# Channel mixing in f16 with the identity folded into the weights, in a sliding-window attention kernel

## The chip, the cores and the metric

The kernel runs on one core of a Trainium2 chip. The metric is the device time of one execution in microseconds (us), the median of several runs. The kernel before takes 632.37 us (3 runs, 632.07 to 632.75).

## The reference

```python
def _attn_ref(q, k, v):                  # 8 batches, 8 heads, 576 tokens, 64 wide
    scores = scale * np.matmul(q, k.transpose(0, 1, 3, 2))
    scores = np.where(mask, scores + bias[None], -1000000000.0)   # band of 128 keys
    ...
    return np.matmul(attn, v)

def _moe_ref(x, w_theta, w_tok_r, w_tok_i, w_ch):                 # x: 8 x 576 x 512
    theta = x @ w_theta
    zr, zi = x * np.cos(theta), x * np.sin(theta)
    y = einsum('ts,bsd->btd', w_tok_r, zr) + einsum('ts,bsd->btd', w_tok_i, zi)
    u = x + y
    return u + np.maximum(u @ w_ch, 0.0)
```

The change concerns the last two lines: u, and the mixing over channels u @ w_ch.

## The kernel before, in words

All data are f32, and each product is made of parts: an operand is split into a high part and the rest (`_hi`, `_lo`), and hi x hi, hi x lo and lo x hi are added up in PSUM. The mixing over tokens uses f16 parts, scaled by powers of two so that they stay in f16's range; the mixing over channels uses f32 parts (type F32R), with no scale.

The work goes by batches. For batch b the main loop calls `attend(b + 1)`, the attention of the next batch, and then `turn(b + 1)`, which turns that attention's result `x_sb` into the tiles `z_hi`, `z_lo`. Between their pieces it places the work that batch b still has:

- `mix` (generator, line 694): mixing over tokens, 8 groups of 27 matmuls 128x288 (in the text: token matmuls). When a group is done, DVE adds it to x (L717, giving u in `xtf`), ACT makes `u_hi` (L719) and POOL makes `u_lo` (L721). The POOL subtractions are kept in `lows` and issued behind the DVE instruction that ends `Head.ready` (L425).
- `channels` (generator, line 737): mixing over channels, 8 **channel groups** of 12 matmuls 128x288: 4 with `wch_hi`,`u_hi`, 4 with `wch_lo`,`u_hi`, 4 with `wch_hi`,`u_lo`. DVE computes max(product, 0) + u (L749) and a DMA writes it out.

`attend` has four steps g = 0 to 3, one per pair of heads. In each, PE computes the scores of a pair four ahead (`ps<-kh,qh`), DVE adds the bias with a custom instruction (L491), ACT takes the exponential (L494), ACT and DVE split the result into f16 parts `hl` (L519, L522), and a DMA transposes them to `pt`. DVE also makes the low parts of the next q and k (L402, L404). PE then multiplies a pair that was prepared before by its values (`ps<-vh,pt`, 54 matmuls), and DVE divides (`finish`, L555 to L560, giving `x_sb`). `turn` transposes `x_sb` (`ps<-fixed,x_sb`, 4 per tile, 5 tiles), splits it (L599 to L606), multiplies by `wth` (theta, 8 or 12 matmuls of 128x512), and DVE, ACT and POOL compute sine, cosine and z.

A channel group is placed at g = 2 and g = 3 of `attend` (for b = 1, the first call, only at g = 3), and six more in `turn`, by `between()`. PE executes its instructions in the program's order (`pinned`); the order on DVE, ACT and POOL comes from a scheduler with a model of the time, so the tables below show it.

The weights of `channels` are loaded late, in `attend(1)`: `unpack(LATE)`, four chunks of 128x512, each decoded (L184 to L193) and split (`split`: ACT L220, POOL L221).

`spread_from` and `spread_to` find the largest value over all partitions: PE transposes a column (L100), DVE takes the maximum and puts it on a diagonal, and PE sends it to all partitions by a matmul with ones. `scales_first` and `batch_scale` derive from it the scales of z.

Of the kernel before, what the change touches and what calls it, by code (L numbers as in the profile page):

```python
# [999 lines left out]
```

## Time and profile before

| what | value |
|---|---|
| median of 3 runs | 632.37 us (632.07 to 632.75) |
| the profiled execution's own time | 630.07 us |
| its span | 628.3 us |
| PE busy | 606.7 us (97%), 5724 matmuls |
| DVE busy | 506.7 us (81%) |
| ACT busy | 482.7 us (77%) |
| POOL busy | 129.9 us (21%) |
| mean granted clock of TensorE | 0.986 of full speed |

The span is from the first to the last instruction; the execution's own time has 1.8 us more. Busy times of different engines overlap. A row of a timeline gives the start in us from the span's beginning, the duration, the engine, the line, the operation, the tiles (out<-in) with partitions and elements, how many instructions it puts together, and in brackets how long the engine had been idle and what ended that. Matmuls are pipelined, so the start of one and the start of the next tell the pace, not the duration of one.

### The profile page before, as it was taken

How to read it: one execution, taken by the hardware profiler on the slowest of the kernel's cores; microseconds unless marked ns; L12 is line 12 of the kernel's file. 1: busy time of each engine (PE TensorE's matmuls, PEld its weight loads, DVE VectorE, ACT ScalarE, POOL GpSimd, SP SyncE). 2: the span in 40 equal slices, each digit the busy share in tenths (PEclk: the TensorE clock that was granted, in tenths of full speed). 3: DMA queues.
4: the chain of work that ended last, by engine and by line, in shares of the span. 5: the costliest groups of instructions: out<-in, count | busy, mean ns of one | idle time of the engine just before them, and what ended most of it. 6: DMA issues, size and time to landing. Idle time of an engine off the chain costs nothing.

```text
span 628.3 us, 14768 instructions
## 1 busy us (share of the span) xinstructions
PE 606.7 (97%) x5724; PEld 522.4 (83%) x5724; DVE 506.7 (81%) x1312; ACT 482.7 (77%) x925; POOL 129.9 (21%) x190
## 2 busy tenths in 40 slices
PE   5898799999999999999999999999999999999997
PEld 3687678879888988889888988889888988898887
DVE  4798888998899879987899879987899769846612
ACT  3998888788988698977988698877997698718600
POOL 4443202320212120210212120220212120121211
PEclk9799889999999999999999999999999999999999
DMA  8971103793079803893089703992088604631001
GB/s 317 356 260 54 34 1 92 177 234 95 29 195 187 177 25 84 194 225 79 20 196 181 185 20 84 202 225 71 20 199 176 146 20 93 102 88 38 10 20 57
DMA packets 137845, 78.09 MB, mean 124 GB/s; under 512 B 110768, under 2 KB 127280, under 8 KB 137776
## 3 DMA queue, kind: packets, MB, share of 16 engines
q1 hardware_dynamic: 137776, 77.15, 50.2%
q8 instruction: 45, 0.74, 0.5%
q14 instruction: 24, 0.20, 0.1%
HBM read 40.44 MB, written 9.44 MB: 79 GB/s over the span
## 4 chain that ended last, share of the span: by engine, by line
PE 45%; DVE 21%; ACT 20%; issue 3%; DMA 2%; POOL 1%; DVEq 0%; ACTq 0%; POOLq 0%; SPq 0%
PE mm L75 36%; PE ps L75 7%; DVE hl L522 3%; ACT front L494 2%; ACT g L633 2%; ACT z_hi L581 2%; ACT hl L519 2%; ACT g L632 2%; ACT back L494 2%; DMA pt<-hl 2%; PE ps L100 2%; DVE f L629 2%; DVE g L642 1%; DVE z_lo L583 1%; ACT xtf L607 1%
## 5 line engine op out<-in xcount | busy, mean ns | idle before, releaser
L75 PE MATMUL mm<-wtk_hi,z_hi 128*128 128x288 f16 x576 | 165.2, 287 | 0.0
L75 PE MATMUL mm<-wtk_lo,z_hi 128*128 128x288 f16 x576 | 164.7, 286 | 0.0
L75 PE MATMUL mm<-wtk_hi,z_lo 128*128 128x288 f16 x576 | 164.7, 286 | 0.0
L75 PEld LDWEIGHTS <-z_hi 128*128 128x128 f16 x1152 | 107.4, 98 | 29.7 <-ACT z_hi L581 0.3
L721 POOL TENSOR_TENSOR u_lo<-xtf,u_hi 128x288 fp32r<-128x288 f32 x64 | 52.7, 839 | 177.2 <-DVE vl L425 74.2
L494 ACT ACTIVATE front<-front,fixed 128x256 f32<-128x256 f32 (+2 forms) x160 | 60.3, 444 | 18.6 <-DVE fixed L491 18.2
L75 PEld LDWEIGHTS <-z_lo 128*128 128x128 f16 x576 | 56.4, 98 | 14.5
L494 ACT ACTIVATE back<-back,fixed 128x256 f32<-128x256 f32 x128 | 56.4, 495 | 2.1 <-DVE fixed L491 2.1
L719 ACT CAST u_hi<-xtf 128x288 fp32r<-128x288 f32 x64 | 26.9, 421 | 34.8 <-DVE xtf L717 34.8
L75 PE MATMUL ps<-kh,qh 64*128 64x256 f32 (+1 forms) x304 | 46.8, 346 | 4.7 <-DVE x_sb L560 3.9
L75 PEld LDWEIGHTS <-pt 128*128 128x128 f16 x1404 | 46.4, 98 | 2.7 <-DMA pt<-hl 1.2
L75 PE MATMUL ps<-vh,pt 128*128 128x65 f16 x936 | 47.6, 194 | 1.0 <-DMA pt<-hl 1.0
L717 DVE SCALAR_TENSOR_TENSOR xtf<-mm,fixed,xtf 128x288 f32<-128x288 f32 x64 | 32.0, 510 | 19.0 <-PE mm L75 19.0
L75 PE MATMUL mm<-wth_hi,x_hi 128*128 128x512 f32 x160 | 47.4, 418 | 0.0
L749 DVE SCALAR_TENSOR_TENSOR xtf<-mm,xtf 128x288 f32<-128x288 f32 x64 | 28.9, 453 | 22.2 <-PE mm L75 21.9
L75 PE MATMUL mm<-u_hi,wch_hi 128*128 128x288 f32 x256 | 46.7, 304 | 0.0
L75 PE MATMUL ps<-vl,pt 128*128 128x64 f16 x468 | 45.9, 193 | 0.0
L75 PE MATMUL mm<-wth_lo,x_hi 128*128 128x512 f32 x160 | 44.9, 402 | 0.0
L75 PE MATMUL mm<-u_hi,wch_lo 128*128 128x288 f32 x256 | 44.5, 295 | 0.0
L75 PE MATMUL mm<-u_lo,wch_hi 128*128 128x288 f32 x256 | 44.4, 295 | 0.0
L642 DVE SCALAR_TENSOR_TENSOR g<-x_sb,fixed,g 128x512 f32<-128x512 f32 x32 | 26.3, 823 | 19.9 <-ACT g L633 19.8
L583 POOL TENSOR_TENSOR z_lo<-g,z_hi 128x512 f16<-128x512 f32 x14 | 16.4, 1170 | 125.0 <-ACT z_hi L581 107.3
(173 smaller groups left out, 1488.9 us busy)
## 6 DMA issues: line engine op xcount, KB each, us to landing
vb<-in_vx_dram SPq DMA_DIRECT2D x16, 650.0 KB, 5.5
out_dram<-xtf SPq DMA_DIRECT2D x64, 144.0 KB, 1.8
qr<-in_qk_dram SPq DMA_DIRECT2D x26, 320.0 KB, 3.4
kr<-in_qk_dram SPq DMA_DIRECT2D x26, 288.0 KB, 3.9
xtf<-in_wch_dram SPq DMA_DIRECT2D x4, 512.0 KB, 4.0
qh<-in_qk_dram SPq DMA_DIRECT2D x6, 320.0 KB, 6.3
kh<-in_qk_dram SPq DMA_DIRECT2D x6, 288.0 KB, 6.6
xtf<-in_wtok_dram SPq DMA_DIRECT2D x3, 576.0 KB, 9.3
```

Source lines behind the costliest of these rows:

```text
L75: ins = nc.tensor.matmul(*args, **kw)
L100: ins = nc.tensor.transpose(*args)
L494: self.exps.append(nc.scalar.activation(sb, sb, AF.Exp, bias=least, scale=-1.0))
L519: self.copied = nc.scalar.activation(hl[:, 0], src, AF.Copy, scale=2.0 ** PEXP)
L522: self.lowered = nc.vector.scalar_tensor_tensor(out=hl[:, 1], in0=src, scalar=2.0 ** PEXP, in1=hl[:, 0], op0=ALU.mult, op1=ALU.subtract)
L581: st["turned"] = nc.scalar.copy(z_hi[:, c, :], z)
L583: low = engine.tensor_tensor(out=z_lo[:, c, :], in0=z, in1=z_hi[:, c, :], op=ALU.subtract)
L642: nc.vector.scalar_tensor_tensor(out=z, in0=x_sb[:, i, :], scalar=zs[:, c:c + 1], in1=z, op0=ALU.mult, op1=ALU.mult)
L717: nc.vector.scalar_tensor_tensor(out=xtf[:, m, cs], in0=y_ps[:, :HALF], scalar=st["back"], in1=xtf[:, m, cs], op0=ALU.mult, op1=ALU.add)
L719: nc.scalar.copy(u_hi[:, m, cs], xtf[:, m, cs])
L721: return nc.gpsimd.tensor_tensor(out=u_lo[:, m, cs], in0=xtf[:, m, cs], in1=u_hi[:, m, cs].bitcast(F32), op=ALU.subtract)
L749: nc.vector.scalar_tensor_tensor(out=xtf[:, e, cs], in0=o_ps[:, :HALF], scalar=0.0, in1=xtf[:, e, cs], op0=ALU.max, op1=ALU.add)
```

## The change

The weights are loaded and decoded into one f32 tile `wch`, the identity is added to the diagonal blocks, and the sums of the rows' absolute values are taken (ACT). In `attend(1)` at g = 3 a scale is found from these sums (`sums_first`, `sums_last`), and `split_channels` makes f16 parts of the whole tile. Since the weights hold the identity, the product is u + u @ w_ch, and the last step is max(product, u). u is scaled by `up` before it is split: ACT scales within the instruction that makes `u_hi`, GpSimd (POOL) makes a scaled copy `us` and subtracts `u_hi` from it, in the last batch DVE does both in one instruction. The evacuation multiplies by `down`. In `attend(1)` no channel group is placed; the following turn takes two at a time instead (`spare`).

```diff
-    wch_hi = const.tile([128, 4, DM], F32R, name="wch_hi")
-    wch_lo = const.tile([128, 4, DM], F32R, name="wch_lo")
+    wch = const.tile([128, 4, DM], F32, name="wch")
+    wch_hi = const.tile([128, 4, DM], F16, name="wch_hi")
+    wch_lo = const.tile([128, 4, DM], F16, name="wch_lo")
...
+            if jobs[k][5] is None:
+                c = jobs[k][3]
+                own = wch[:, c, c * 128:c * 128 + 128]
+                nc.vector.tensor_tensor(out=own, in0=own, in1=ident, op=ALU.add)
+                nc.scalar.activation(ex.bitcast(F32), wch[:, c, :], AF.Abs, scale=2.0 ** -(WEXP - 1),
+                                     accum_out=csums[:, c:c + 1])
...
-            elif scale is None:
-                nc.scalar.copy(hi[:, c, :], val)
-                nc.gpsimd.tensor_tensor(out=lo[:, c, :], in0=val, in1=hi[:, c, :].bitcast(F32), op=ALU.subtract)
...
+        up = rings["up"].take()
+        nc.gpsimd.tensor_scalar(out=up, in0=t, scalar1=ratio[:, :1], scalar2=None, op0=ALU.mult)
...
+    def sums_first():
+
+        nc.vector.tensor_reduce(out=peaks[1][:, :1], in_=csums, axis=mybir.AxisListType.X, op=ALU.max)
+        nc.vector.tensor_scalar(out=peaks[1][:, :1], in0=peaks[1][:, :1], scalar1=2.0 ** (WEXP - 1),
+                                scalar2=2.0 ** -100, op0=ALU.mult, op1=ALU.max)
+        return spread_from(peaks[1], 1, "c")
+
+    def sums_last(diag):
+
+        s = spread_to(diag, 1, "c")
+        nc.vector.tensor_scalar(out=ratio[:, 1:2], in0=ratio[:, :1], scalar1=s, scalar2=None, op0=ALU.mult)
+        inverse(ratio[:, 2:3], ratio[:, 1:2])
+        return s
+
+    def split_channels(s):
+
+        for k in range(0, 4, 2):
+            part = slice(k, k + 2)
+            nc.scalar.activation(wch_hi[:, part], wch[:, part], AF.Copy, scale=s)
+            nc.vector.scalar_tensor_tensor(out=wch_lo[:, part], in0=wch[:, part], scalar=s, in1=wch_hi[:, part],
+                                           op0=ALU.mult, op1=ALU.subtract)
...
-                nc.scalar.copy(u_hi[:, m, cs], xtf[:, m, cs])
-                def low(m=m, cs=cs):
-                    return nc.gpsimd.tensor_tensor(out=u_lo[:, m, cs], in0=xtf[:, m, cs],
-                                                   in1=u_hi[:, m, cs].bitcast(F32), op=ALU.subtract)
-
+                nc.scalar.activation(u_hi[:, m, cs], xtf[:, m, cs], AF.Copy, scale=up)
                 if st["b"] + 1 < B:
-                    lows.append(low)
+                    nc.gpsimd.tensor_scalar(out=us[:, m, cs], in0=xtf[:, m, cs], scalar1=up, scalar2=None, op0=ALU.mult)
+                    lows.append(lambda m=m, cs=cs: nc.gpsimd.tensor_tensor(
+                        out=u_lo[:, m, cs], in0=us[:, m, cs], in1=u_hi[:, m, cs], op=ALU.subtract))
                 else:
-                    low()
+                    nc.vector.scalar_tensor_tensor(out=u_lo[:, m, cs], in0=xtf[:, m, cs], scalar=up, in1=u_hi[:, m, cs],
+                                                   op0=ALU.mult, op1=ALU.subtract)
...
+        down = rings["down"].take()
+        nc.gpsimd.tensor_scalar(out=down, in0=st["back"], scalar1=ratio[:, 2:3], scalar2=None, op0=ALU.mult)
...
-                nc.vector.scalar_tensor_tensor(out=xtf[:, e, cs], in0=o_ps[:, :HALF], scalar=0.0, in1=xtf[:, e, cs],
-                                               op0=ALU.max, op1=ALU.add)
+                nc.vector.scalar_tensor_tensor(out=xtf[:, e, cs], in0=o_ps[:, :HALF], scalar=down, in1=xtf[:, e, cs],
+                                               op0=ALU.mult, op1=ALU.max)
...
+            if b == 1 and g == 3:
+                diag = sums_first()
             step(mixing, steps[2])
             pair.values()
...
-            if g >= 2 and (b > 1 or g == 3):
+            if g >= 2 and b > 1:
                 step(chans)
+            if b == 1 and g == 3:
+                s = sums_last(diag)
+                with tc.issue_after(done.ins):
+                    split_channels(s)
...
-            turn(x_sb, st[b + 1])(lambda: step(chans))
+            spare = [0, 0, 2, 2, 2] if b == 0 else []
+            turn(x_sb, st[b + 1])(lambda: step(chans, spare.pop(0) if spare else 1))
```

On PE the order is the same in both kernels outside `attend(1)`, g = 3, and the turn behind it. The first place is PE between the scores of that step and its values: token matmuls stand there in a row before (L75 is the helper that records every matmul; L77 in the changed kernel).

```order
L75 MATMUL mm<-wtk_lo,z_hi 128x288
L75 LDWEIGHTS z_lo
L75 MATMUL mm<-wtk_hi,z_lo 128x288
L75 LDWEIGHTS z_hi
L75 MATMUL mm<-wtk_hi,z_hi 128x288
```

and now

```order
L77 MATMUL mm<-wtk_lo,z_hi 128x288
L77 LDWEIGHTS z_lo
L77 MATMUL mm<-wtk_hi,z_lo 128x288
L102 MATMUL mm<-fixed,peak_104 128x128
L77 LDWEIGHTS z_hi
L77 MATMUL mm<-wtk_hi,z_hi 128x288
```

The new matmul is the transpose of the column `peak` that `sums_first` fills; 12 token matmuls stand between the scores and it, 12 more and the 54 of the values come behind it.

The second place is PE from the end of that step's token matmuls into the turn, before:

```order
L75 MATMUL mm<-wtk_hi,z_lo 128x288
L75 MATMUL mm<-u_hi,wch_hi 128x288 x4
L75 MATMUL mm<-u_hi,wch_lo 128x288 x4
L75 MATMUL mm<-u_lo,wch_hi 128x288 x4
L75 MATMUL mm<-u_hi,wch_hi 128x288 x4
L75 MATMUL mm<-u_hi,wch_lo 128x288 x4
L75 MATMUL mm<-u_lo,wch_hi 128x288 x4
L100 MATMUL ps<-fixed,x_sb 128x128 x4
L75 MATMUL mm<-u_hi,wch_hi 128x288 x4
L75 MATMUL mm<-u_hi,wch_lo 128x288 x4
L75 MATMUL mm<-u_lo,wch_hi 128x288 x4
L100 MATMUL ps<-fixed,x_sb 128x128 x4
```

and now

```order
L77 MATMUL mm<-wtk_hi,z_lo 128x288
L77 MATMUL mm<-fixed 128x1
L102 MATMUL ps<-fixed,x_sb 128x128 x8
L77 MATMUL mm<-wth_hi,x_hi 128x512 x4
L77 MATMUL mm<-wth_lo,x_hi 128x512 x4
L77 LDWEIGHTS wch_hi
L77 MATMUL mm<-u,wch_hi 128x288
```

The three channel groups that stood ahead of and between the first transposes have gone behind the first theta, where two now stand together, as they do at the two places after it; eight are left for the turn and its end.

The third place is DVE at that step, from the low parts of q and k on, before:

```order
L402 SCALAR_TENSOR_TENSOR ql<-qr,qh 128x640
L404 TENSOR_TENSOR kl<-kr,kh 128x576
L717 SCALAR_TENSOR_TENSOR xtf<-mm,fixed,xtf 128x288
L522 SCALAR_TENSOR_TENSOR hl<-front_101,hl 128x1024
L555 SCALAR_TENSOR_TENSOR fixed<-ps,fixed 128x10
```

and now, there

```order
L439 SCALAR_TENSOR_TENSOR ql<-qr,qh 128x640
L441 TENSOR_TENSOR kl<-kr,kh 128x576
L347 TENSOR_REDUCE peak_104<-fixed 128x1
L756 SCALAR_TENSOR_TENSOR xtf<-mm,fixed,xtf 128x288
L348 TENSOR_SCALAR peak_104<-peak_104 128x1
L559 SCALAR_TENSOR_TENSOR hl<-front_101,hl 128x1024
L313 TENSOR_REDUCE fixed<-mm 128x1
```

and behind the step's end

```order
L158 TENSOR_SCALAR fixed<-mm 128x1
L637 TENSOR_TENSOR x_hi<-ps,x_hi 128x4x64
L643 TENSOR_TENSOR x_lo<-ps,x_hi 128x512
L160 TENSOR_SCALAR fixed<-fixed 128x1
L297 TENSOR_REDUCE peak_104<-vb 128x4
L355 TENSOR_SCALAR fixed<-fixed 128x1
L165 TENSOR_SCALAR fixed<-fixed 128x1
L364 SCALAR_TENSOR_TENSOR wch_lo<-wch,fixed,wch_hi 128x1024 x2
```

The two instructions that fill the column (L347, L348) stand behind the low parts of q and k and around a token group's evacuation; the scale (L158, L160) and the low parts of the weights (L364) stand behind the turn's first splits and a reduction of the values (L297, which is L291 before).

## Rows read from the trace of the kernel before

**Rows 1.** The page, busy times: engine, us, share of the span, instructions.
```profile
PE 606.7 (97%) x5724; PEld 522.4 (83%) x5724; DVE 506.7 (81%) x1312; ACT 482.7 (77%) x925; POOL 129.9 (21%) x190
```

**Rows 2.** The chain of waits in time order, one batch (b = 4): start, us, what.
```profile
353.89 1.60 PE mm L75 x12
...
400.88 0.83 DVE x_sb L560
401.85 0.98 PE ps L75 x12
```

**Rows 3.** Timeline of PE where a batch's first long scores begin.
```profile
260.75 0.39 PE L75 MATMUL ps<-kh,qh 64*128 64x256 f32 x2 [0.39 <-DVE x_sb L560]
```

**Rows 4.** Stretches: window, us, PE, PEld, DVE, ACT, POOL busy, clock, DMA, GB/s.
```profile
165.90:208.90 43.00, 43.00 (x558) 36.78 (x556) 41.52 (x129) 35.50 (x71) 5.61 (x14) 1.00 0.72 174
```

**Rows 5.** Timeline of PE: 12 token matmuls, and one channel group of 12.
```profile
132.68 0.29 PE L75 MATMUL mm<-wtk_hi,z_hi 128*128 128x288 f16 x1
...
134.15 0.19 PE L75 MATMUL ps<-vh,pt 128*128 128x65 f16 x1
...
139.19 0.70 PE L75 MATMUL mm<-u_hi,wch_hi 128*128 128x288 f32 x4
...
140.78 0.92 PE L100 MATMUL ps<-fixed,x_sb 128*128 128x128 f32 x4
```

**Rows 6.** Timeline of DVE in `attend(1)`, g = 3, and the turn behind it.
```profile
136.02 0.74 DVE L404 TENSOR_TENSOR kl<-kr,kh 128x576 fp32r<-128x576 f32 x1
136.69 0.50 DVE L717 SCALAR_TENSOR_TENSOR xtf<-mm,fixed,xtf 128x288 f32<-128x288 f32 x1
...
145.01 1.48 DVE L291 TENSOR_REDUCE peak<-vb 128x4 f32<-128x1280 f32 x1
```

**Rows 7.** Timeline of PE, same place: values, theta, channels, next tokens.
```profile
135.19 0.20 PE L75 MATMUL ps<-vh,pt 128*128 128x65 f16 x1 [0.52 <-DMA pt<-hl]
...
136.49 0.29 PE L75 MATMUL mm<-wtk_hi,z_hi 128*128 128x288 f16 x1
...
143.50 1.19 PE L75 MATMUL mm<-wth_hi,x_hi 128*128 128x512 f32 x4
...
145.45 0.69 PE L75 MATMUL mm<-u_hi,wch_hi 128*128 128x288 f32 x4
...
150.28 0.70 PE L75 MATMUL mm<-u_hi,wch_hi 128*128 128x288 f32 x4
...
165.94 0.30 PE L75 MATMUL mm<-wtk_hi,z_hi 128*128 128x288 f16 x1
```

**Rows 8.** Groups by line and form: busy us, mean ns of one, idle before.
```profile
L522 DVE SCALAR_TENSOR_TENSOR hl<-front,hl 128x1024 f16<-128x1024 f32 x26 | 32.0, 1229 | 1.9 <-ACT hl L519 1.9
L519 ACT ACTIVATE hl<-front 128x1024 f16<-128x1024 f32 x26 | 27.1, 1043 | 0.5 <-DMA pt<-hl 0.5
L387 POOL TENSOR_SCALAR ql<-ql 128x512 f32<-128x512 f32 x5 | 8.2, 1644 | 6.6 <-DMA ql<-in_band_dram 4.1 <-DVE fixed L491 2.4
L749 DVE SCALAR_TENSOR_TENSOR xtf<-mm,xtf 128x288 f32<-128x288 f32 x64 | 28.9, 453 | 22.2 <-PE mm L75 21.9
```

**Rows 9.** Timeline of POOL and DVE: instructions that run beside each other, two places.
```profile
163.24 1.17 POOL L583 TENSOR_TENSOR z_lo<-f,z_hi 128x512 f16<-128x512 f32 x1
163.88 1.08 DVE L642 SCALAR_TENSOR_TENSOR g<-x_sb,fixed,g 128x512 f32<-128x512 f32 x1 [1.63 <-ACT g L633]
164.88 0.74 DVE L642 SCALAR_TENSOR_TENSOR f<-x_sb,fixed,f 128x512 f32<-128x512 f32 x1
...
59.91 1.72 POOL L214 TENSOR_SCALAR wtk_hi<-u_hi,fixed 128x576 f16<-128x576 f32 x1 [7.41 <-DVE fixed L553]
60.92 0.75 DVE L191 SCALAR_TENSOR_TENSOR u_lo<-u_lo 128x576 int32<-128x576 int32 x1
```

**Rows 10.** Stretches, columns as in rows 4: a pause of PE and what followed.
```profile
71.80:75.20 3.40, 1.60 (x13) 1.15 (x11) 3.37 (x8) 3.37 (x6) 0.00 (x0) 1.00 0.10 13
75.20:82.00 6.80, 5.53 (x14) 4.46 (x15) 5.78 (x17) 3.96 (x7) 0.65 (x1) 0.50 0.20 70
```

More of the change, by code (lines that the diff above doesn't have):

```diff
@@ L40 @@
 RINGS = ([("mx", 2 * NT, 4)] + [("den", 2 * NT, 3)] + [("whole", 1, 2), ("vs", 2 * GROUP, 2), ("scale", 2 * GROUP, 2)]
-         + [("whole0", 1, 1), ("vs0", 13, 1), ("scale0", 13, 1), ("sum", 9, 1),
-            ("row", 9, 1), ("inv", 9, 1), ("lim", 1, 1), ("t", 1, 2), ("zs", 9, 2), ("back", 1, 2)])
+         + [("whole0", 1, 1), ("vs0", 14, 1), ("scale0", 14, 1), ("sum", 9, 1),
+            ("row", 9, 1), ("inv", 9, 1), ("lim", 1, 1), ("t", 1, 2), ("zs", 9, 2), ("back", 1, 2)]
+         + [("wholec", 1, 1), ("vsc", 2 * GROUP, 1), ("scalec", 2 * GROUP, 1), ("sumc", 4, 1), ("ratio", 3, 1),
+            ("up", 1, 2), ("down", 1, 2)])
 LOWS = float(np.float32(2.0 ** -29 * (1.0 - 2.0 ** -19)))
@@ L51, in attn_moe_kernel @@
 @with_exitstack
-def attn_moe_kernel(ctx: ExitStack, tc: tile.TileContext, qk_in, vx, wth, wtok, wch, band, out):
+def attn_moe_kernel(ctx: ExitStack, tc: tile.TileContext, qk_in, vx, wth, wtok, wch_in, band, out):
     nc = tc.nc
@@ L135, in attn_moe_kernel @@
     wth_lo = const.tile([128, 4, DM], F32R, name="wth_lo")
-    wch_hi = const.tile([128, 4, DM], F32R, name="wch_hi")
-    wch_lo = const.tile([128, 4, DM], F32R, name="wch_lo")
+    wch = const.tile([128, 4, DM], F32, name="wch")
+    wch_hi = const.tile([128, 4, DM], F16, name="wch_hi")
+    wch_lo = const.tile([128, 4, DM], F16, name="wch_lo")
     wtk_hi = const.tile([128, 9, S], F16, name="wtk_hi")
     wtk_lo = const.tile([128, 9, S], F16, name="wtk_lo")
-    sums, rows, invs, lim = (rings[name].take() for name in ("sum", "row", "inv", "lim"))
+    sums, rows, invs, lim, csums, ratio = (rings[name].take() for name in ("sum", "row", "inv", "lim", "sumc", "ratio"))
     qr = const.tile([128, S + 64], F32, name="qr")
@@ L192, in together @@
                                            op1=ALU.bitwise_or)
-            nc.vector.scalar_tensor_tensor(out=b, in0=z, scalar=-0x80000000, in1=b,
+            ex, whole = z, b if jobs[k][5] is not None else wch[:, jobs[k][3], :].bitcast(I32)
+            nc.vector.scalar_tensor_tensor(out=whole, in0=z, scalar=-0x80000000, in1=b,
                                            op0=ALU.bitwise_and, op1=ALU.bitwise_or)
-            ex = z
+            if jobs[k][5] is None:
[4 more added lines that the diff above has]
+                                     accum_out=csums[:, c:c + 1])
             if jobs[k][5] == "row":
@@ L232, in unpack @@
             for k in range(n):
-                for fn in (apart, together, split):
-                    fn(k, t)
+                apart(k, t)
+                together(k, t)
                 if k + 1 < n:
@@ L260, in attn_moe_kernel @@
             + [(wtok, wtk_hi, wtk_lo, c, S, "row") for c in ORDER])
-    LATE = [(wch, wch_hi, wch_lo, c, DM, None) for c in range(4)]
+    LATE = [(wch_in, None, None, c, DM, None) for c in range(4)]
     def load_pair(p):
@@ L294, in add_up @@
     def add_up(g, to):
-        flat = wch_lo.rearrange("p c n -> p (c n)")[:, :GROUP * NT * 64]
+        flat = wch.rearrange("p c n -> p (c n)")[:, :GROUP * NT * 64]
         nc.scalar.activation(flat.rearrange("p (c d) -> p c d", d=64),
@@ L696, in mix @@
         xtf, z_hi, z_lo = st["xtf"], st["z_hi"], st["z_lo"]
-        u_hi = big.tile([128, 4, S], F32R, name="u_hi")
-        u_lo = big.tile([128, 4, S], F32R, name="u_lo")
+        u = big.tile([128, 2, 4, S], F16, name="u")
+        us = big.tile([128, 4, S], F32, name="us")
+        u_hi, u_lo = u[:, 0], u[:, 1]
         st.update(u_hi=u_hi, u_lo=u_lo)
+        up = u_scale[st["b"]]
         banks = {}
@@ L896, in attn_moe_kernel @@
     x_sb = xp.tile([128, NT, DM], F32, name="x_sb")
-    kept = unpack(JOBS, ((uf, "xtf"), (uf, "xtf"), (big, "z_hi"), (big, "z_lo"), (big, "u_hi"), (big, "u_lo")))
+    kept = unpack(JOBS, ((uf, "xtf"), (uf, "xtf"), (big, "z_hi"), (big, "z_lo"), (big, "u"), (big, "us")))
     last, done = start(x_sb, kept)
```

14 lines of the change are left out of this document (10 added, 4 removed).

## The prediction, made before the change was run

> **What bounds the kernel now.** I read the page's busy times first: PE is busy for 606.7 of 628.3 us [rows 1], so nearly everything that shortens PE's work seems to be worth its time. The chain of waits says less. In each batch it lies on PE up to the turn's second group of transposes (the last PE piece starts at 353.89 and takes 1.60 us, to 355.49), and from there for some 45 us on ACT and DVE in turn, until DVE's `x_sb` lets PE start the scores of the next batch's third step at 401.85 [rows 2]. PE is filled with other work in that time, and all that it waits there is a fraction of a us: the matmul at 260.75 had to wait for `x_sb`, 0.39 us [rows 3], and alike in the later batches. So two paths of nearly equal length run beside each other: PE, and a path through ACT and DVE. In batch 2's `attend` DVE is busy for 41.52 of 43.00 us while PE has no pause at all [rows 4]. From PE's work only what lies in the PE part of the chain shortens a batch; the rest turns into a longer wait for `x_sb`. A change below 0.2% (1.3 us) can't be told from none.
>
> **The gain.** A channel group takes 140.78 - 139.19 = 1.59 us in f32 parts; 12 token matmuls of the same size in f16 take 134.15 - 132.68 = 1.47 us [rows 5]. The new channel matmuls have the form of the latter, so I take 0.12 us per group, 64 x 0.12 = 7.7 us in all if every group counted. Of the 8 groups of a batch 4 stand in the PE part of the chain (one at g = 2, two around the end of g = 3, one ahead of the second transposes): 4 x 0.12 = 0.48 us per batch that count, 0.48 that go into the wait.
>
> **Batch 1, the new wait.** The new transpose stands on PE behind 12 token matmuls, so PE comes to it at 132.68 [rows 5]. Its column is ready late: DVE gets to L347 and L348 only behind the custom instructions of this step's scores and the low parts of q and k. In the trace before, the last of these starts at 136.02 and ends by 136.69, and the evacuation that stands between the two takes 0.50 [rows 6]. With about 0.2 for the added 128x128 sum ahead of them and 0.3 for the two small ones (both estimates, against the 0.50 of a 128x288) the transpose starts at about 137.65. PE stands still for 5.0 us, and all that is queued behind the transpose stands with it: 12 token matmuls, the values, the turn. I replay it:
> - 12 token matmuls to 139.1; the values, 136.49 - 134.15 = 2.34 us before with a pause of 0.52 for `pt` [rows 7] that is over by now, so 1.8, to 140.9; 9 token matmuls, to 142.0. `x_sb` is ready at about 142.2, the 8 transposes end at 142.8, and after the splits the first theta starts at 143.7 (143.50 before) and ends 145.45 - 143.50 = 1.95 later [rows 7], at 145.65. That theta is nearly on time because the three channel groups ahead of it are gone.
> - Then PE wants `wch_hi`, `wch_lo`. ACT makes `wch_hi` in two pieces of 128x1024, 1.04 us each [rows 8], behind the turn's first copies: 146.15 and 147.1. DVE makes `wch_lo` behind the 1.48 us of the reduction [rows 6], two pieces of 1.23 [rows 8]: 147.4 and 148.6. The first channel group so ends at 149.4, 2.3 us later than its matmuls need; the second at 150.9. The transposes and the second theta take 150.28 - 145.45 - 1.59 = 3.24 [rows 5, 7], so that theta ends at 154.1 instead of 150.28.
> - Behind that stood 15.66 us up to the next token matmuls (165.94 - 150.28 [rows 7]) with 4 channel groups. Now there are 6: 15.66 + 2 x 1.47 - 4 x 0.12 = 18.1, to 172.2. That is **+6.3 us** against 165.94, this batch's gain in f16 included. In batch 2 PE had no pause [rows 4], so nothing takes it up. Bounds: 4.5 if the column comes 1 us sooner and `wch_lo` too, 7.5 if both come later.
>
> **The clock.** Where PE was busy for 1.60 of 3.40 us, the granted clock in the next 6.80 us was 0.50, the lower of its two levels, 1.2 GHz [rows 10]; PE worked 5.53 us in it, which would be about 2.8 at 2.4 GHz, so 2.8 us is what one such fall can cost. The new wait is as long a pause, with matmuls at once behind it. Some of the slower time falls into the wait for `wch_lo`. I take **+2.0** (0 to 5, the upper end for two falls).
>
> **Every batch, beside the gain.**
> - POOL's `us`, 56 times 128x288: no row has this form. By elements L387 gives 1644 x 288/512 = 925 ns [rows 8], L583, with two inputs, 1.17 x 288/512 = 0.66 us [rows 9]; I take 0.93, the same operation, together 52 us more on an engine with 129.9 busy [rows 1]. It stands ahead of `u_lo` and of the small memsets of `vh`; the channel groups that need it come steps later, so I cost the delay at nothing. If that cover fails, a channel group waits about 1 us per batch.
> - DVE beside POOL: L642 took 1.08 us under a POOL instruction and 0.74 alone; L191 took 0.75 under one with a scalar pointer, as `us` has, and lost nothing [rows 9]. Two of a batch's eight `us` fall on DVE's `hl` splits in the ACT and DVE part of the chain: 0 to 0.34 each, taken at 0.2, together 0.4.
> - The evacuation of a channel group gets a scalar pointer, which makes its form that of L717: 0.51 instead of 0.453 [rows 6, 8], 0.06 more; 2 of the 8 lie on DVE's path, +0.12.
> - Sum per batch: -0.48 + 0.12 + 0.4 = +0.04. Over the five batches of this kind **+0.2** (-0.36 to +0.3 each, -1.8 to +1.5). In batch 2, where PE had no wait, up to 0.96 counts: **-0.7**. At the end nothing but PE counts: 4 groups in the last turn, 8 behind it, 0.3 from DVE's `u_lo` in place of POOL's: -0.48 - 0.96 - 0.3 = **-1.7**.
> - What goes from the weights' chunks (ACT's copy, POOL's subtraction) lies beside the scores of `attend(1)`, where PE was not waiting for them: nothing.
>
> The GPSIMD Engine Reference of the Trainium skill, in "4.1 Engine selection", holds POOL instructions with one input to run at about line rate and only those with two to be about twice as slow as on VectorE. Here L387, with one input, takes 1.64 us for 128x512 [rows 8], and L583, with two, 1.17 [rows 9], so the trace does not bear it out. By that rule `us` would be shorter than `u_lo` and hide entirely, and the sum would be 2.0 us lower.
>
> **Sum.** +6.3 + 2.0 + 0.2 - 0.7 - 1.7 = +6.1. The profiled execution took 630.07 us, 2.3 below the median of 632.37; I carry the difference over to the median: **638.5 us**.
>
> **Rivals.**
> - *PE decides everywhere* (the other side: faster). If DVE's path has slack that the rows do not show, so that PE's wait before the third step does not grow, each of the 56 groups outside batch 1 counts: -6.7 - 0.3. This decides from the point at which `x_sb` is ready 0.5 us before PE needs it. For it: PE is 97% busy [rows 1] and the wait is only 0.39 [rows 3]. Against it: a wait is there in every batch from the third on, and DVE gets more to do. With +6.3 for batch 1 and no fall of the clock it gives 632.4 + 6.3 - 7.0 = 631.7; with the lower bound of the wait, 4.5, 629.9. Middle 630.8.
> - *DVE is held up by POOL, and the clock falls twice.* Each `us` costs the full 0.34 or runs into the next split: +0.3 per batch, 1.5; clock +5.0. 632.4 + 6.3 + 5.0 + 1.5 - 0.7 - 1.7 = 642.8. For it: 1.08 against 0.74 [rows 9] and a DVE with 1.5 us free [rows 4]. Against it: the L191 row. The GPSIMD Engine Reference of the Trainium skill, "1. Specifications", says that GpSimd shares its SBUF interfaces with VectorE and that instructions of VectorE with two SBUF inputs contend; `hl` has two, so by that rule this rival is the likelier, but the rows of this case go both ways.
> - *No fall of the clock*: the forecast without 2.0, 636.5. For it: the values and the tokens behind the wait run without another pause.
> - *The f16 form brings nothing*: the channel groups keep 1.59 because the pace is not set by the type. Then 0.48 per batch and the ends' gains go, about +5: 643.5. Against it: rows 5 are the same size on the same engine.
>
> **How the numbers follow.** Forecast 0.38, no fall of the clock 0.17, PE decides 0.23, held up by POOL 0.18, f16 brings nothing 0.04. Of the 0.23, 0.13 lies under 631.1 (faster), 0.08 within 0.2%; a shorter batch 1 together with no fall adds 0.03 to each. So faster 0.16, same 0.11, slower 0.73. The range that leaves out about 2 in 10 goes from 630.5 to 643.5.
>
> **What would show it.** The timeline of PE in `attend(1)`, g = 3: a pause of about 5 us ahead of one transpose, ended by DVE, and a second of about 2.3 in pieces ahead of the first channel groups. The granted clock at 0.5 behind the first. Channel groups of 1.47. From the third batch on a wait for `x_sb` of about 0.39 + 0.48 + 0.52 = 1.4 us, and a period as before. POOL busy near 180 us, with `us` at 0.93. The prediction is wrong if the pause is under 3 us, if the wait for `x_sb` does not grow (then PE decides), or if `hl` splits beside `us` take over 1.5 us.

## The result, and the profile after

The changed kernel takes 635.91 us (median of 9 runs, 634.16 to 637.26), the kernel before 632.42 us on the same chips (9 runs, 631.67 to 634.48). The ratio is 1.0052, 95% interval 1.0037 to 1.0068: slower, by 2.3 to 4.3 us. The forecast was 638.5, with a range of 630.5 to 643.5. The profiled execution of the changed kernel has a span of 634.1 us and its time is the median; that of the kernel before had been 2.3 us below its own.

Of the page of the changed kernel, the busy times, which answer to [rows 1]:

```profile
PE 600.8 (95%) x5727; PEld 493.0 (78%) x5727; DVE 519.2 (82%) x1336; ACT 491.0 (77%) x931; POOL 198.8 (31%) x251
```

PE is busy 5.9 us less, and the kernel is slower. To see where, I cut both executions at the same places of PE's order: the first score matmul of `attend(1)`'s steps g = 2 and g = 3, of `attend(2)`'s g = 0, of `attend(3)`'s g = 1 and of `attend(7)`'s g = 1. Stretches of the kernel before (window, us, then PE, PEld, DVE, ACT and POOL busy, granted clock, DMA share, GB/s):

```profile
118.43:128.33 9.90, 9.90 (x135) 8.43 (x133) 9.87 (x28) 6.89 (x16) 4.49 (x6) 1.00 1.02 275
128.33:168.43 40.10, 38.98 (x310) 34.27 (x308) 34.23 (x72) 34.04 (x63) 9.99 (x11) 1.00 0.48 112
168.43:248.26 79.83, 79.83 (x853) 69.44 (x851) 70.98 (x191) 66.59 (x126) 11.94 (x21) 1.00 0.55 126
248.26:529.78 281.52, 279.66 (x2862) 243.09 (x2862) 245.78 (x640) 234.94 (x446) 47.22 (x80) 1.00 0.58 130
529.78:628.30 98.52, 94.67 (x847) 82.10 (x845) 51.74 (x121) 43.76 (x85) 17.47 (x23) 1.00 0.27 57
```

The same stretches of the changed kernel:

```profile
120.76:131.78 11.02, 10.07 (x135) 8.48 (x133) 10.54 (x32) 7.61 (x16) 4.97 (x7) 1.00 1.12 251
131.78:179.00 47.22, 40.35 (x314) 31.24 (x311) 37.49 (x80) 36.57 (x66) 14.93 (x15) 0.96 0.38 93
179.00:258.92 79.92, 78.91 (x853) 65.50 (x851) 72.19 (x191) 68.24 (x127) 25.24 (x33) 1.00 0.54 127
258.92:537.89 278.97, 275.13 (x2863) 227.06 (x2862) 247.64 (x640) 235.89 (x446) 92.44 (x121) 1.00 0.60 131
537.89:634.10 96.21, 92.33 (x847) 74.74 (x845) 56.15 (x128) 45.07 (x84) 19.31 (x24) 1.00 0.29 59
```

Up to the first of these places the changed kernel has lost 2.33 us (120.76 against 118.43); the rows then give +1.12, **+7.12**, +0.09, **-2.55** (four batches, 0.64 each) and **-2.31**. The 2.33 is not put down to the change: five executions of kernels that have the start of the kernel before come to that place between 117.22 and 120.87 us. In their first 117 us the mean granted clock is between 0.90 and 0.96, highest in the one that comes first. Without the 2.33 the sum is +3.47, and the medians say +3.49.

The +7.12 is the step that the forecast was about. All that PE waits for in the stretch around it, in the changed kernel (engine, line, what it waited for: us in total, times, longest):

```profile
PE mm L102 <- DVE peak L348: 4.4, 1, 4.4
PE mm L77 <- DVE x_hi L637: 1.0, 1, 1.0
PE ps L77 <- DMA pt<-hl: 1.0, 1, 1.0
PE mm L77 <- DVE wch_lo L364: 0.8, 1, 0.8
PE mm L77 <- ACT wch_hi L363: 0.6, 1, 0.6
```

and in the kernel before:

```profile
PE ps L75 <- DMA pt<-hl: 0.5, 1, 0.5
PE ps L75 <- DVE x_sb L560: 0.5, 1, 0.5
```

The pause is there and is ended by L348. On PE's timeline of the changed kernel the transpose, the late theta, two channel groups, and a wait that is new in later batches read so:

```profile
139.91 0.33 PE L102 MATMUL mm<-fixed,peak 128*128 128x128 f32 x1 [4.38 <-DVE peak L348]
...
148.09 1.20 PE L77 MATMUL mm<-wth_hi,x_hi 128*128 128x512 f32 x4 [0.97 <-DVE x_hi L637]
...
158.36 0.66 PE L77 MATMUL mm<-u,wch_hi 128*128 128x288 f16 x4
...
161.31 0.60 PE L102 MATMUL ps<-fixed,x_sb 128*128 128x128 f32 x4
...
323.74 0.30 PE L77 MATMUL mm<-wtk_hi,z_lo 128*128 128x288 f16 x1 [1.00 <-DVE z_lo L620]
```

From 158.36 to 161.31 there are two channel groups: 2.95 us, 1.475 each, as the token matmuls of [rows 5] said. The last row stands for five of its kind: PE now waits for the last `z_lo` of a batch, and the wait of [rows 3] for `x_sb` is gone. DVE's order explains that: three of its score instructions stand between the last two `z_lo`, where in the kernel before there was one. The changed kernel's DVE at that place:

```profile
321.37 0.69 DVE L620 TENSOR_TENSOR z_lo<-g,z_hi 128x512 f16<-128x512 f32 x1
...
321.97 0.41 DVE L528 CUSTOM_DVE_ANT_0 back<-ps,bands 128x256 f32<-128x256 f32 x1
...
322.31 0.42 DVE L528 CUSTOM_DVE_ANT_0 back<-ps,bands 128x256 f32<-128x256 f32 x1
...
322.66 0.42 DVE L528 CUSTOM_DVE_ANT_0 back<-ps,bands 128x256 f32<-128x256 f32 x1
...
323.00 0.68 DVE L620 TENSOR_TENSOR z_lo<-f,z_hi 128x512 f16<-128x512 f32 x1
```

### The profile page after: what moved, and what is told of

Same layout as the page of the kernel before. It is cut to its first block, busy times and chain, and to the rows that moved or that the text cites. A ratio compares the mean times of both kernels' runs of the same rounds, so it can differ in the third digit from the quotient of the medians.

```text
span 634.1 us, 14879 instructions
## 1 busy us (share of the span) xinstructions
PE 600.8 (95%) x5727; PEld 493.0 (78%) x5727; DVE 519.2 (82%) x1336; ACT 491.0 (77%) x931; POOL 198.8 (31%) x251
## 4 chain that ended last, share of the span: by engine, by line
PE 57%; ACT 18%; DVE 18%; DMA 4%; issue 2%; SPq 0%; DVEq 0%; ACTq 0%
PE mm L77 43%; PE ps L77 13%; DMA pt<-hl 3%; ACT g L670 2%; DVE z_lo L620 2%; ACT g L669 2%; PE ps L102 2%; ACT z_hi L618 2%; DVE f L666 2%; DVE front L528 1%; DVE g L679 1%; DVE peak L297 1%; ACT back L531 1%; ACT front L531 1%; ACT xtf L644 1%
## 5 line engine op out<-in xcount | busy, mean ns | idle before, releaser
L77 PE MATMUL mm<-wtk_hi,z_lo 128*128 128x288 f16 x576 | 165.4, 287 | 4.6 <-DVE z_lo L620 4.6
L77 PE MATMUL mm<-wtk_hi,z_hi 128*128 128x288 f16 x576 | 165.6, 287 | 0.0
L77 PE MATMUL mm<-wtk_lo,z_hi 128*128 128x288 f16 x576 | 165.3, 287 | 0.0
L77 PEld LDWEIGHTS <-z_hi 128*128 128x128 f16 x1152 | 109.0, 98 | 29.6 <-issue 0.6
L760 POOL TENSOR_SCALAR us<-xtf,fixed 128x288 f32<-128x288 f32 x56 | 73.0, 1306 | 106.7 <-DVE xtf L756 101.5
L77 PE MATMUL mm<-u,wch_hi 128*128 128x288 f16 x512 | 81.8, 287 | 0.7 <-ACT wch_hi L363 0.6
L77 PEld LDWEIGHTS <-z_lo 128*128 128x128 f16 x576 | 56.5, 98 | 20.4 <-DVE z_lo L620 6.1
L77 PEld LDWEIGHTS <-wch_hi 128*128 128x128 f16 x512 | 47.8, 98 | 19.8 <-issue 7.4
L758 ACT ACTIVATE u<-xtf,fixed 128x288 f16<-128x288 f32 x64 | 33.5, 525 | 33.3 <-DVE xtf L756 33.3
L761 POOL TENSOR_TENSOR u<-us,u 128x288 f16<-128x288 f32 x56 | 42.2, 769 | 48.7 <-DVE vl L462 24.0
L77 PE MATMUL ps<-vh,pt 128*128 128x65 f16 x936 | 48.0, 195 | 1.9 <-DMA pt<-hl 1.9
L77 PEld LDWEIGHTS <-pt 128*128 128x128 f16 x1404 | 46.9, 98 | 3.8 <-DMA pt<-hl 2.4
L77 PE MATMUL mm<-wth_hi,x_hi 128*128 128x512 f32 x160 | 47.5, 419 | 1.9 <-DVE x_hi L637 1.4
L77 PE MATMUL ps<-kh,qh 64*128 64x256 f32 (+1 forms) x304 | 46.7, 348 | 1.2 <-DVE fixed L528 0.7
L77 PE MATMUL ps<-vl,pt 128*128 128x64 f16 x468 | 46.1, 193 | 0.0
L77 PE MATMUL mm<-wth_lo,x_hi 128*128 128x512 f32 x160 | 44.5, 399 | 0.0
L77 PE MATMUL mm<-u,wch_lo 128*128 128x288 f16 x256 | 42.0, 286 | 0.8 <-DVE wch_lo L364 0.8
```

The source lines that it names most:

```text
L77: ins = nc.tensor.matmul(*args, **kw)
L758: nc.scalar.activation(u_hi[:, m, cs], xtf[:, m, cs], AF.Copy, scale=up)
L760: nc.gpsimd.tensor_scalar(out=us[:, m, cs], in0=xtf[:, m, cs], scalar1=up, scalar2=None, op0=ALU.mult)
L761: lows.append(lambda m=m, cs=cs: nc.gpsimd.tensor_tensor(out=u_lo[:, m, cs], in0=us[:, m, cs], in1=u_hi[:, m, cs], op=ALU.subtract))
```

## The experiments

Two questions were open. Is a batch's length set by PE, or by PE's part of the chain and ACT and DVE behind it, so that half of the f16 gain is worth nothing? And is the loss all made in batch 1, or do the scaling of u and POOL's copies cost something in every batch? Nine kernels were run. The column "four batches" is the stretch from `attend(3)`'s second scores to `attend(7)`'s second scores, as in the fifth rows above; it has no part in batch 1 or in the start. The kernel before was run again beside the others, with medians of 631.45 to 632.26 us, so the ratios compare better than the medians. Each figure of the last column is from one execution. The change, no_sums, sums_late and filled do the same work in these batches and take 278.74 to 279.29, so a difference under about 0.6 us says nothing.

| kernel | median us | ratio to the kernel before (95%) | four batches, us |
|---|---|---|---|
| before | 632.42 | 1 | 281.52 |
| the change | 635.91 | 1.0052 (1.0037 to 1.0068) | 278.97 |
| f16_only | 627.05 | 0.9921 (0.9906 to 0.9936) | 279.21 |
| no_us | 636.21 | 1.0060 (1.0038 to 1.0082) | 278.31 |
| no_sums | 629.21 | 0.9962 (0.9944 to 0.9980) | 278.86 |
| z_first | 636.80 | 1.0076 (1.0055 to 1.0097) | 278.52 |
| sums_late | 631.93 | 0.9998 (0.9980 to 1.0016) | 278.74 |
| filled | 634.51 | 1.0034 (1.0014 to 1.0054) | 279.29 |
| f16_zpool | 625.29 | 0.9897 (0.9869 to 0.9924) | 279.05 |
| f16_one | 624.09 | 0.9872 (0.9851 to 0.9894) | 277.80 |
| f16_two | 625.26 | 0.9884 (0.9864 to 0.9904) | 278.55 |

**f16_only: the gain alone.** The kernel before, and in it:

```diff
-    wch_hi = const.tile([128, 4, DM], F32R, name="wch_hi")
-    wch_lo = const.tile([128, 4, DM], F32R, name="wch_lo")
+    wch_hi = const.tile([128, 4, DM], F16, name="wch_hi")
+    wch_lo = const.tile([128, 4, DM], F16, name="wch_lo")
...
-        u_hi = big.tile([128, 4, S], F32R, name="u_hi")
-        u_lo = big.tile([128, 4, S], F32R, name="u_lo")
+        u = big.tile([128, 2, 4, S], F16, name="u_hi")
+        u_hi, u_lo = u[:, 0], u[:, 1]
```

> The kernel before, with the parts of u and of the channel weights in f16 and nothing else: no scale, no identity, no sums, the old places of the channel groups (what it leaves out is the scaling). Theory of the two paths (only the 4 of 8 channel groups in the PE part of a batch count): 6 x 0.48 + 0.48 + 0.96 = 4.3 us less than before, about 628.1 us, with the wait for x_sb ahead of a batch's third scores grown from 0.4 to about 0.9 us. Rival, PE decides everywhere: 64 x 0.12 = 7.7 us less, 624.7, and that wait unchanged. Rival, the form brings nothing: 632.4 with channel groups of 1.59 us.

Measured 627.05 us, a ratio of 0.9921: 4.0 to 5.9 us less. That holds the 4.3 of the two paths and leaves out both the 7.7 of PE alone and the "nothing". The four batches are

```profile
249.88:529.09 279.21, 276.75 (x2863) 227.34 (x2862) 245.47 (x640) 234.74 (x446) 44.95 (x80) 1.00 0.59 131
```

2.31 us shorter than before, 0.58 per batch (0.48 expected), though PE's busy time in a batch fell by 0.73 (279.66 - 276.75 over four). Cut by steps, g = 3 with its turn goes from 37.45 to 36.62 us, 0.12 for each of its seven channel groups, and the g = 0 behind it from 10.35 to 10.77. The wait for `x_sb` did not grow as I had expected; its row in this kernel's waits is as before (1.7 us in 5 times):

```profile
PE ps L75 <- DVE x_sb L561: 1.6, 5, 0.4
```

What PE gained beyond that became waits for `z_lo` (0.8 us, new) and for `pt` (1.2 us, before 0.4, the longest in batch 2). So a part of the gain is lost behind another chain, as the theory says, but at another place than it says.

**no_us: POOL's copies alone.** The changed kernel without the scaling of u's low part, and in it:

```diff
-                    nc.gpsimd.tensor_scalar(out=us[:, m, cs], in0=xtf[:, m, cs], scalar1=up, scalar2=None, op0=ALU.mult)
                     lows.append(lambda m=m, cs=cs: nc.gpsimd.tensor_tensor(
-                        out=u_lo[:, m, cs], in0=us[:, m, cs], in1=u_hi[:, m, cs], op=ALU.subtract))
+                        out=u_lo[:, m, cs], in0=xtf[:, m, cs], in1=u_hi[:, m, cs], op=ALU.subtract))
```

> The changed kernel without POOL's scaled copy: the subtraction takes u itself (the scaling of the low part is left out). Theory: POOL beside DVE makes some of DVE's splits longer, 0.2 to 0.4 us per batch on the path: 1.5 to 2.5 us less than the changed kernel, about 634. Rival, it is hidden: within 0.5 of 635.9. Rival, the copies hold up u_lo and with it channel groups: the waits of PE for u would be seen in the changed kernel; none is, so nothing from this.

Measured 636.21 us against 635.91, and over the four batches

```profile
260.61:538.92 278.31, 274.76 (x2864) 226.90 (x2862) 246.81 (x640) 236.25 (x446) 47.02 (x88) 1.00 0.59 131
```

0.66 us less than the change, 0.17 per batch, at half the POOL time (47.02 instead of 92.44), and hardly more than such batches differ by. So POOL's copies are hidden but for 0.17 at most; my 0.4 per batch was too much. The profile says why. `hl` on DVE and `us` on POOL in the changed kernel's groups (busy us, mean ns, idle before):

```profile
L760 POOL TENSOR_SCALAR us<-xtf,fixed 128x288 f32<-128x288 f32 x56 | 73.0, 1306 | 106.7 <-DVE xtf L756 101.5 <-DVE peak L348 4.1 <-DVE fixed L325 0.5
...
L559 DVE SCALAR_TENSOR_TENSOR hl<-front,hl 128x1024 f16<-128x1024 f32 x26 | 31.7, 1220 | 2.0 <-ACT hl L556 1.9
L559 DVE SCALAR_TENSOR_TENSOR hl<-back,hl 128x1024 f16<-128x1024 f32 x26 | 33.2, 1275 | 5.5 <-ACT hl L556 5.2
```

`hl<-front` takes 1220 ns, before 1229 [rows 8]; `hl<-back` 1275, before 1221: eight of the 52 splits took 1.35 to 1.50 us, about one in a batch. `us` takes 1306 ns in the mean where I had put 0.93 us. The two engines do hold each other up, but POOL waits far more than DVE (more in the last section).

**no_sums: the change without the weights' own scale.** Each chunk is split when it is decoded, and the channel groups of `attend(1)` and the turn are where they were:

```diff
+                c = jobs[k][3]
+                nc.scalar.copy(wch_hi[:, c, :], wch[:, c, :])
+                nc.gpsimd.tensor_tensor(out=wch_lo[:, c, :], in0=wch[:, c, :], in1=wch_hi[:, c, :], op=ALU.subtract)
...
-            if b == 1 and g == 3:
-                diag = sums_first()
...
-            if g >= 2 and b > 1:
+            if g >= 2 and (b > 1 or g == 3):
                 step(chans)
-            if b == 1 and g == 3:
-                s = sums_last(diag)
-                with tc.issue_after(done.ins):
-                    split_channels(s)
```

> The changed kernel without the weights' own scale: no sums, no transpose, no pause; each chunk is split to f16 by ACT and POOL where it was before, the identity added, and the channel groups back in their old places. All that a batch has of the change stays: f16, the scaling of u by ACT and POOL, the pointer in the evacuation, the maximum. Theory: the whole loss of the changed kernel is made in the second batch and the rest of the change costs nothing: 627 to 628, like f16_only. Rival: the scaling of u, the evacuation and POOL's copies cost 0.4 to 0.6 us per batch: 630.

Measured 629.21 us, 6.7 less than the change, and 2.2 more than f16_only. The rival's 630 is nearer than the theory's 627 to 628, but not for the rival's reason. The stretches of this kernel, the step ahead of batch 1's last, and that last step with its turn:

```profile
121.42:133.03 11.61, 10.09 (x135) 8.50 (x133) 11.27 (x32) 8.15 (x17) 6.02 (x7) 1.00 1.13 247
133.03:172.61 39.58, 37.78 (x310) 30.36 (x308) 34.35 (x69) 32.37 (x60) 14.33 (x14) 1.00 0.47 110
```

The four batches take 278.86, no more than f16_only's 279.21, with scaling, pointers, maximum and POOL's copies all in them. The last step with its turn takes 39.58 (f16_only: 39.14). Most of what is left of the loss is the 11.61 against 9.90 of the step ahead, where PE waits for the transfer that brings `pt`; the change has 11.02 there. That step varies: 9.90 to 9.92 us in all five executions of the kernel before and of f16_only and its variants, but 9.90, 9.91, 10.40, 11.02, 11.63 and 11.61 in those of the change and its variants, of which sums_late (9.90) and the change (11.02) have the same DVE instructions there, at the same durations. The DMA engines are full in that step (share 1.02 to 1.13), so what differs is when `pt` lands; why stays open.

**sums_late: the transpose behind the values.** The changed kernel, and in it:

```diff
-            if b == 1 and g == 3:
-                diag = sums_first()
             step(mixing, steps[2])
             pair.values()
             with tc.high_priority(FINISH):
                 done = pair.finish(x_sb)
+            if b == 1 and g == 3:
+                diag = sums_first()
...
-            spare = [0, 0, 2, 2, 2] if b == 0 else []
-            turn(x_sb, st[b + 1])(lambda: step(chans, spare.pop(0) if spare else 1))
+            spare = [0, 0, 0, 3, 3] if b == 0 else []
+
+            def between():
+                if len(spare) == 4:
+                    split_channels(sums_last(diag))
+                step(chans, spare.pop(0) if spare else 1)
+
+            turn(x_sb, st[b + 1])(between)
```

> The changed kernel, with the transpose for the weights' scale put behind the values of that step instead of 12 token matmuls behind its scores, the scale and the split behind the turn's first transposes, and the channel groups of that turn behind its second theta (three at a time). Theory: the pause of 4.4 us, the fall of the clock behind it (about 1.5) and the wait for the f16 weights (1.4) go, and about 1 us of new waits comes for x_sb and the scale: 5 to 6 us less than the changed kernel, 630 to 631, and no clock of 0.5 after 82 us. Rival, DVE is the bound of this batch and PE only waits elsewhere: 1 to 2 us less, 634.5, with a pause of 3 us or more in the turn.

Measured 631.93 us, 4.0 less than the change: between the theory's 5 to 6 and the rival's 1 to 2. The stretch that took 47.22 us takes

```profile
130.14:174.29 44.15, 39.41 (x314) 30.75 (x311) 38.11 (x83) 36.59 (x67) 14.11 (x15) 1.00 0.46 102
```

so 3.07 come from it, of which the next experiment puts 1.63 down to the clock, which stayed at 1.00; the step ahead is 1.12 shorter. Of the pause of 4.4 little is won: its waits moved on, to

```profile
PE mm L77 <- DVE x_hi L637: 1.9, 1, 1.9
PE mm L102 <- DVE peak L348: 1.1, 1, 1.1
PE ps L102 <- DVE x_sb L597: 0.6, 1, 0.6
PE ps L77 <- DVE x_sb L597: 0.6, 1, 0.6
```

4.2 us in these four, each ended by DVE, which is busy for 38.11 of the 44.15 us. So the rival is half right: much of what PE does not wait for at one place it waits for at the next. No wait is as long as the 3 us that it named.

**filled: the clock alone.** The changed kernel with work for PE in the pause:

```diff
             if b == 1 and g == 3:
+                unread(new.scored, 38)
                 diag = sums_first()
```

> The changed kernel with 38 matmuls of 128x256 that nobody reads ahead of the new transpose, so that PE works through the pause (about 4 us) and ends with it. Theory: the clock behind the pause stays at 1.0, and the 12 token matmuls and the values behind it take 1.5 and 1.7 us instead of 2.7 and 2.1: 1.3 to 1.7 us less at the next batch's scores, 634.5. Rival: DVE is the bound there too, x_sb comes no sooner than before, and the time comes back as a wait: less than 0.5, 635.9.

Measured 634.51 us, 1.4 less; the intervals overlap, so the stretches decide. The first 3.4 us behind the pause, in the changed kernel,

```profile
140.30:143.70 3.40, 3.40 (x30) 2.46 (x28) 2.32 (x4) 2.67 (x4) 1.56 (x1) 0.50 0.86 239
```

in this kernel the whole stretch:

```profile
133.63:178.79 45.16, 42.66 (x351) 33.99 (x349) 37.06 (x80) 35.91 (x66) 14.52 (x15) 1.00 0.41 96
```

and its transpose and first theta:

```profile
141.35 0.32 PE L102 MATMUL mm<-fixed,peak 128*128 128x128 f32 x1
147.90 1.21 PE L77 MATMUL mm<-wth_hi,x_hi 128*128 128x512 f32 x4 [0.97 <-DVE x_hi L637]
```

With PE kept busy the clock stays at 1.00 instead of falling to 0.50, and 47.22 becomes 45.16. Not all of the 2.06 is the clock's. From the transpose to the theta it is 147.90 - 141.35 = 6.55 us instead of 148.09 - 139.91 = 8.18: the fall cost 1.63 us here. Most of the rest lies ahead of the transpose, which comes 7.72 us behind the step's first matmul instead of 8.13, after a step ahead that was 0.61 longer. The theory is right, the rival out. In the executions of no_us and z_first the same way took 8.89 and 8.72 us, so there a fall cost 2.3 and 2.2.

**z_first: the new wait for `z_lo`.** The changed kernel, and in it:

```diff
-                    with tc.issue_after(lowered.ins) if b == 1 and g == 0 else nullcontext():
+                    with tc.issue_after(lowered.ins) if g == 0 and (b == 1 or tiles == SCORES[2]) else nullcontext():
                         new.scores(tiles, behind)
```

> The changed kernel, with DVE's instructions for the last four score tiles of a batch's first step ordered behind the last z_lo. Theory: the pause of 1.0 us that PE has before z_lo in each batch falls to about 0.2, but the path through DVE and ACT is as long as before, so half of it comes back as a wait for x_sb ahead of the third scores: 6 x 0.4 = 2.4 us less than the changed kernel, about 633.5. Rival, the pause is PE's own loss: 6 x 1.0 less, 630. Rival, the DVE path is what counts: no change, 635.9.

Measured 636.80 us: no gain. PE's five waits of 1.0 us for `z_lo` are gone, and in their place stands

```profile
PE mm L77 <- DVE fixed L315: 1.8, 5, 0.4
```

and the four batches take 278.52 us, 0.45 less than in the change, which is within what such batches differ by. The third expectation was right: PE's wait there is not what makes a batch long. (The batch 1 of this execution was 1.6 us longer than the change's, with a longer fall of the clock.)

**f16_zpool, f16_one, f16_two: is it ACT and DVE?** All build on f16_only. f16_zpool moves two subtractions per batch from DVE to POOL:

```diff
-                    split_z(c, z, nc.gpsimd if st["b"] and i < 3 else nc.vector)
+                    split_z(c, z, nc.gpsimd if st["b"] and i < 4 else nc.vector)
```

and f16_one and f16_two move in addition ACT's copies of one or two tiles to DVE (`{3}`, `{2, 3}`):

```diff
-            nc.scalar.copy(xtf[:, :, t0:t0 + n], x_ps.rearrange("p (c t) -> p c t", t=128))
+            (nc.vector.tensor_copy if st["b"] and i in (3,) else nc.scalar.copy)(
+                xtf[:, :, t0:t0 + n], x_ps.rearrange("p (c t) -> p c t", t=128))
```

> The kernel f16_only with the z_lo of the fourth tile of a turn on POOL too (two subtractions of 0.68 us less on DVE per batch, two of 1.17 more on POOL). Theory: the path through ACT and DVE sets a batch's length, so a shorter DVE makes it shorter: 0.4 to 1.0 us per batch, 2 to 5 in all, 622 to 625. Rival: DVE is not the bound, or POOL's z_lo comes too late and PE waits for it: 627 or above, with a wait of PE for z_lo by POOL.

> The kernel f16_zpool with one of a turn's copies of x to xtf (tile 3, 0.58 us) on DVE instead of ACT, from the second batch on. Theory: in f16_only ACT and DVE are two paths of the same length behind PE's part, so a shorter DVE alone gave nothing; with both shorter (ACT 0.58, DVE 1.36 - 0.6) a batch gets 0.4 to 0.6 us shorter, until PE's own time is the bound: the wait for x_sb goes from 0.4 to 0 and 2 to 3 us in all, 622.5 to 623.5. Rival, ACT's copy is not on the path: the batches keep f16_zpool's length, 625.3.

> As f16_one, with the copies of tiles 2 and 3 on DVE (ACT 1.16 us shorter, DVE as long as in f16_only). Theory: no better than f16_one, since DVE is then as long as before and PE has no more wait to give: 623 to 625. Rival, only ACT counts: 0.5 us per batch less than f16_one, 620 to 621.

The four batches of the first two, in this order, each from its own execution:

```profile
246.33:525.38 279.05, 276.94 (x2862) 227.41 (x2862) 241.13 (x632) 234.57 (x446) 54.12 (x88) 1.00 0.59 131
```

```profile
249.09:526.89 277.80, 276.69 (x2862) 227.79 (x2862) 243.28 (x636) 233.58 (x442) 54.09 (x88) 1.00 0.59 132
```

f16_zpool: DVE is 4.3 us less busy over four batches (245.47 to 241.13), and the batches are as long as f16_only's (279.21). So DVE by itself is not the bound, and the theory of that expectation fell. The chain of waits shows what took DVE's place. Behind a turn it lies on DVE in f16_only and has gone over to ACT in f16_zpool:

```profile
383.18 0.60 DVE z_lo L584
```

```profile
379.03 1.28 ACT L495
```

(Its median is 1.8 us below f16_only's, at overlapping intervals and with the difference in the start, so I don't count it.) f16_one: with ACT 1.2 us less busy as well, the four batches are 1.41 us shorter than f16_only's, and the median is 624.09, with an interval that does not touch f16_only's (f16_zpool's it does). Between 165 and 615 us only one wait of PE is left:

```profile
PE ps L75 <- DVE x_sb L561: 0.3, 1, 0.3
```

So in this kernel PE itself is nearly all of what makes a batch long. f16_two: four copies more go from ACT to DVE, the four batches take 278.55, and the gain is half lost again, since PE now waits for DVE:

```profile
PE mm L75 <- DVE z_lo L584: 5.4, 4, 1.3
```

This fits two chains of nearly one length, one with more of ACT in it and one with more of DVE: taking from one gives nothing, from both a little, and loading one with the other's work takes it back. The moves also change the order on both engines; no run separates that. The gain of f16_one, 0.35 us per batch, is smaller than the 0.4 to 0.6 expected, and its 624.09 us more than the 622.5 to 623.5. f16_one beats both kernels, by 1.1 to 1.5% against the kernel before; like f16_only it leaves out the scaling of u and of the weights, which the change has for data that f16's range would not hold.

## Why the prediction was right, and where it was not

- **The size of the f16 gain** was right: 1.475 us per channel group, forecast 1.47. **That only a part of it counts** was right too: 0.58 per batch in f16_only, forecast 0.48, and about 4.9 in all instead of 7.7. But where the rest goes was wrong. It was to become a longer wait for `x_sb`, and the prediction said that it is wrong if this wait does not grow, since then PE decides. In f16_only it stayed (1.6 us, before 1.7), in the change it is gone, and still PE does not decide: the rest went into the wait for `z_lo`, 0.8 and 4.6 us.
- **The pause in batch 1** was right in place, cause and order of size: 4.38 us, ended by L348, forecast 5.0. The wait for the f16 weights was 0.8 + 0.6 = 1.4, forecast 2.3. Theta started 148.09 - 139.91 = 8.2 us behind the transpose, forecast 6.05: the slow clock (1.63), and 1.0 of waiting for `x_hi`, which stands on DVE behind `x_sb`, two `vl` and an evacuation. So there was less left to wait.
- **The clock**: 1.63 in this execution, 2.2 and 2.3 in two others, forecast 2.0.
- **The chunks "nothing"** holds for the change, though the step ahead of the pause took 1.12 us longer, by a wait for `pt`. The pause takes that up, since DVE sets when it ends: the transpose starts 139.91 - 120.76 = 19.15 us behind the first matmul of step g = 2, and 140.95 - 121.80 = 19.15 in z_first, where that step took 9.91 us (forecast 137.65 - 118.43 = 19.22). In no_sums, which has no such pause, the same kind of wait was paid, and why it comes in some executions is open. Both steps together are 7.12 + 1.12 = 8.24 longer, 6.6 without the clock; forecast 8.3 and 6.3. So the small misses, theta later, the weights and the clock cheaper, cancel.
- **"Every batch, beside the gain"** is the step that failed: +0.4 from POOL's copies and +0.12 from the evacuation, so that batches would keep their length. Four batches got 2.55 us shorter, 0.64 each, forecast +0.04. No_us and no_sums show that the two terms are all but off the path: 0.17 per batch at most without the copies, and nothing between no_sums (278.86), which has both, and f16_only (279.21). That is the chief reason why the kernel came out 2.6 us faster than forecast; the direction did not hang on it, since the loss is made in batch 1. Batch 2 gave nothing (+0.09, forecast -0.7), where PE has waits now that it did not have (78.91 us busy of 79.92, before all of 79.83); the end gave -2.31, forecast -1.7.
- **The rivals.** "PE decides everywhere" is refuted by f16_only's interval. "DVE is held up by POOL" wanted 0.7 per batch and 5.0 for the clock; no_us leaves 0.17, and the clock cost 1.63. The Trainium skill's GPSIMD Engine Reference, "1. Specifications", is right that the two contend, and the trace agrees (1.91 us of `us` beside `hl`, 1.01 without), but the one held up was mostly POOL, which has the time. Its "4.1 Engine selection", that one input runs at about line rate, the trace does not bear out: `us` takes 1.01 us undisturbed, longer than the subtraction with two inputs of the same size in the same timeline (0.73).

## What to carry to other kernels

A short operation that PE must wait for is dear by what stands ahead of it on the engine that makes it: find that engine's order, and place the matmul behind the work that PE has anyway, and then look whether the wait only moves to the next thing that this engine makes. Where PE is 97% busy and another chain has almost the same length, a saving on PE counts only in part, since PE then waits for the other chain, and not always where it waited before; a saving on one engine of the other chain may count for nothing until its partner is relieved too. A cost beside other engines should be placed on the engine that actually waits: here 69 us more on POOL cost 0.17 us a batch at most, since it was mostly POOL that was held up.

## What the runs showed of the hardware

POOL's and DVE's instructions beside each other, in the changed kernel. POOL's timeline at three places:

```profile
335.59 0.30 POOL L340 TENSOR_SCALAR fixed<-fixed 128x1 f32<-128x1 f32 x1 [2.94 <-DVE fixed L336]
...
336.99 1.90 POOL L778 TENSOR_SCALAR fixed<-fixed 128x1 f32<-128x1 f32 x1
...
345.63 1.91 POOL L760 TENSOR_SCALAR us<-xtf,fixed 128x288 f32<-128x288 f32 x1 [3.12 <-DVE xtf L756]
...
348.86 1.01 POOL L760 TENSOR_SCALAR us<-xtf,fixed 128x288 f32<-128x288 f32 x1 [1.22 <-DVE xtf L756]
...
356.64 1.90 POOL L760 TENSOR_SCALAR us<-xtf,fixed 128x288 f32<-128x288 f32 x1 [4.36 <-DVE xtf L756]
```

and DVE's at the same times:

```profile
337.58 1.22 DVE L559 SCALAR_TENSOR_TENSOR hl<-back,hl 128x1024 f16<-128x1024 f32 x1
...
345.45 1.21 DVE L559 SCALAR_TENSOR_TENSOR hl<-front,hl 128x1024 f16<-128x1024 f32 x1
...
357.62 1.50 DVE L559 SCALAR_TENSOR_TENSOR hl<-back,hl 128x1024 f16<-128x1024 f32 x1
```

A POOL instruction of one element per partition took 1.90 us where another took 0.30: it began under one `hl` split (336.45 to 337.66) and ended with the next, at 338.8. `us` beside an `hl` that had begun before it took 0.90 us longer than alone, and the `hl` took its usual 1.21. All 19 `us` that began under a running `hl` took 1.67 us or more. The other way round DVE pays less and not always: of the 25 `hl` that began under a `us`, those with up to 0.6 us of it left took 1.20 to 1.23, and the eight with 0.78 to 0.92 left took 1.35 to 1.50, as the one at 357.62 did. In [rows 9], L642, which began under a running POOL instruction, took 1.08 instead of 0.74. Which of several DVE forms do this was not tried.
